# How many loads are issued ahead of the entry barriers in a streaming scale-and-add kernel: three or one

## The chip, the cores and the metric

The kernel runs on one core of one Trainium2 chip. Times are device microseconds of one execution; where a run was timed, the median of its executions is given beside that of the kernel before on the same chip. The profile of an execution counts from the first instruction to the last (the span), and was about 1.3 us shorter than the measured time of the same execution.

## The reference

```python
# x, y: [1024, 16, 512] bf16; gamma: [512] bf16
def reference(x, y, gamma):
    return x + gamma * y
```

Each of x, y and the output is 16.78 MB. Seen as 128 partitions, each partition has 128 rows of 512 elements, 1 KB a row.

## The kernel before

y and x are each loaded in halves of 64 rows per partition. x's buffer in this kernel has 75 rows. Its first half takes 64 of them. The second half comes in two loads: 53 rows overwrite rows of the first half and must wait until VectorE has added these (below, this is "the reload"); the last 11 rows go to a place of their own, but stand behind the reload in the queue. The two queues are written as lists: SP issues loads, ACT issues gamma and the two stores.

```python
PIECES = [53, 11, 53, 11]
SP = [('y', 0, 64), ('x', 0, 64, 0), ('y', 64, 128), ('x', 64, 117, 0), ('x', 117, 128, 64)]
ACT = [('g',), ('s', 0, 64), ('s', 64, 128)]
EARLY = (2, 1)          # how many of SP's and of ACT's issues go ahead of the entry barriers
RELEASE = ('x', 64, 117, 0)
DVE = [('m', 0), ('m', 1), ('a', 0), ('a', 1), ('m', 2), ('m', 3), ('a', 2), ('a', 3)]
```

gamma arrives as one row of 1 KB, is spread to 128 partitions by a matmul with a row of ones, and cast by VectorE:

```python
    nc.vector.memset(ones_row, 1.0).then_inc(s_ones, 1)
    _take(s_ones, 1, nc.tensor)
    _take(s_gamma, 16, nc.tensor)
    nc.tensor.matmul(gamma_ps, ones_row, gamma_row, start=True, stop=True).then_inc(s_ps, 1)
    _take(s_ps, 1, nc.vector)
    nc.vector.tensor_copy(out=gamma_sb, in_=gamma_ps).then_inc(s_dve, 1)
    # ... then VectorE multiplies ('m') and adds ('a') piece by piece
```

At the end of the build, the first issues of each queue are moved to the front of the program, ahead of the barriers that the framework puts at its entry:

```python
            if k < n_early:
                early.append(i.ins)
    # ...
    for k, i in enumerate(early):
        main.insert(1 + k, i)
```

## Time and profile before

| | |
|---|---|
| time, three runs | 119.91 us (119.9 to 120.03) |
| span of the profiled run | 118.6 us |
| both DMA queues, share of 16 engines | 66.0% + 32.6% |
| VectorE busy | 70.0 us, 59% |
| 64 KB packets | 2.418 us each, 48 packets' worth on each DMA engine |

The packets of the two queues fill 98.6% of the 16 engines' span, and VectorE, the busiest of the others, works 59% of it: DMA is the bound. The prediction below shows the page's head and the timeline of the start. The view of waits of the kernel before says who has time to spare. Its columns are: engine, tile and line; what it waited for; us in total, how many times, the longest.

```profile
DVE y_sb L156 <- DVEq L25: 15.4, 2, 13.4
PE gamma_ps L130 <- PEq L25: 7.1, 1, 7.1
...
DVE y_sb L165 <- DVEq L25: 2.2, 1, 2.2
```

L156 is the multiply, L165 the add, L130 the matmul for gamma; L25 is the helper that waits on a semaphore. The first multiply waited 13.4 us although gamma was there, and the first add 2.2 us for x.

### The profile page before, as it was taken

The page shows a single profiled execution, that of the slowest core. Times are in us where ns is not written, and L with a number is a line of the kernel's source. Part 1 is how long each engine was busy: PE and PEld are TensorE (multiplying, and loading weights), DVE is VectorE, ACT ScalarE, POOL GpSimd, SP SyncE. Part 2 cuts the span into 40 slices and gives each one's busy share as a digit, 9 for nine tenths or more (in the row PEclk, how much of TensorE's full clock was granted, in tenths as well). Part 3 has the DMA queues.
Part 4 walks back from the last instruction along what each step waited for, and adds up shares of the span by engine and source line. Part 5 has one row for each costly group of instructions (what it writes and reads, how often), then busy time and mean ns, then how long its engine had stood idle before and what let it go on. Part 6 is the DMA issues. An engine that isn't in the chain of part 4 may idle for free. (4 is left out here: it accounts for less than half of the span.)

```text
span 118.6 us, 78 instructions
## 1 busy us (share of the span) xinstructions
PE 0.6 (0%) x1; PEld 0.1 (0%) x1; DVE 70.0 (59%) x10; POOL 0.2 (0%) x4
## 2 busy tenths in 40 slices
PE   0010000000000000000000000000000000000000
PEld 0000000000000000000000000000000000000000
DVE  0020000699999299999759999999999910000000
POOL 0000000000000000000000000000000000000000
DMA  9889888998899888988896969498899888988892
GB/s 354 354 376 685 354 354 354 641 420 354 354 420 641 354 354 354 685 376 354 354 586 293 586 293 568 201 658 354 354 420 641 354 354 354 708 354 354 354 597 111
DMA packets 1010, 50.33 MB, mean 425 GB/s; under 512 B 113, under 2 KB 114, under 8 KB 114
## 3 DMA queue, kind: packets, MB, share of 16 engines
q1 hardware_dynamic: 720, 33.55, 66.0%
q10 hardware_dynamic: 290, 16.78, 32.6%
HBM read 33.56 MB, written 16.78 MB: 425 GB/s over the span
## 5 line engine op out<-in xcount | busy, mean ns | idle before, releaser
L156 DVE TENSOR_TENSOR y_sb<-y_sb,gamma_sb 128x27136 bf16<-128x27136 bf16 (+1 forms) x4 | 34.6, 8688 | 15.4 <-DVEq L25 15.4
L165 DVE TENSOR_TENSOR y_sb<-x_sb,y_sb 128x27136 bf16<-128x27136 bf16 (+1 forms) x4 | 34.6, 8689 | 2.3 <-DVEq L25 2.2
L132 DVE CAST gamma_sb<-gamma_ps 128x512 bf16<-128x512 f32 x1 | 0.7, 691 | 5.7 <-DVEq L25 5.7
L127 DVE MEMSET ones_row<- 1x128 bf16 x1 | 0.2, 165 | 2.0 <-PEq L41 2.0
L130 PE MATMUL gamma_ps<-gamma_row,ones_row 1*128 1x512 bf16 x1 | 0.6, 580 | 7.1 <-PEq L25 7.1
L130 PEld LDWEIGHTS gamma_ps<-gamma_row,ones_row 1*128 1x128 bf16 x1 | 0.1, 100 | 7.1 <-issue 7.1
L194 POOL MEMSET const-bfloat16-1.0<- 128x1 bf16 x1 | 0.1, 101 | 0.0
L194 POOL MEMSET const-uint8-127<- 128x1 uint8 x1 | 0.1, 101 | 0.0
L194 POOL MEMSET const-float32-0.0<- 128x1 f32 x1 | 0.1, 98 | 0.2 <-issue 0.2
L194 POOL MEMSET const-float32-1.0<- 128x1 f32 x1 | 0.1, 98 | 0.0
## 6 DMA issues: line engine op xcount, KB each, us to landing
x_sb<-in_x_dram SPq DMA_DIRECT2D x1, 6784.0 KB, 20.8
x_sb<-in_x_dram SPq DMA_DIRECT2D x1, 1408.0 KB, 23.8
y_sb<-in_y_dram SPq DMA_DIRECT2D x2, 40.2
out_dram<-y_sb ACTq DMA_DIRECT2D x2, 22.7
gamma_row<-in_gamma_dram ACTq DMA_DIRECT2D x1, 1.0 KB
x_sb<-in_x_dram SPq DMA_DIRECT2D x1, 40.7
```

Of the source, the lines that this page charges most:

```text
L127: nc.vector.memset(ones_row, 1.0).then_inc(s_ones, 1)
L130: nc.tensor.matmul(gamma_ps, ones_row, gamma_row, start=True, stop=True).then_inc(s_ps, 1)
L132: nc.vector.tensor_copy(out=gamma_sb, in_=gamma_ps).then_inc(s_dve, 1)
L156: nc.vector.tensor_tensor(out=yt, in0=yt, in1=g, op=MULT).then_inc(s_dve, 1)
L165: nc.vector.tensor_tensor(out=yt, in0=xt, in1=yt, op=ADD).then_inc(s_add, 1)
L194: nc = _bacc.Bacc("TRN2", target_bir_lowering=False, num_devices=1)
```

## The change

The intent is to keep only what the start needs ahead of the barriers: the first load of y. x's first load and gamma are issued behind them.

```diff
-EARLY = (2, 1)
+EARLY = (1, 0)
```

y's first load is 64 rows of 1 KB on each of 128 partitions, 8.39 MB. By the code of the build, the programs differ only in the place of two DMA instructions (both profiles count 78 instructions): x's load on SP and gamma's on ACT now stand behind the barriers.

## The prediction

> **What bounds the kernel now.** I read the page's head first, then its busy rows, its DMA queues, and the timeline.
>
> ```profile
> span 118.6 us, 78 instructions
> ...
> PE 0.6 (0%) x1; PEld 0.1 (0%) x1; DVE 70.0 (59%) x10; POOL 0.2 (0%) x4
> ...
> DMA  9889888998899888988896969498899888988892
> ...
> q1 hardware_dynamic: 720, 33.55, 66.0%
> q10 hardware_dynamic: 290, 16.78, 32.6%
> HBM read 33.56 MB, written 16.78 MB: 425 GB/s over the span
> ```
>
> The two DMA queues together keep the 16 DMA engines busy for 66.0 + 32.6 = 98.6% of the span; only 1.4% of 118.6 us, about 1.7 us, is free. VectorE, the busiest compute engine, works 59%. So DMA is the bound, and a change of order can save no more than that 1.7 us unless it changes the traffic, which it doesn't. What it can do is open a gap in the traffic. The timeline of the first 10 us shows the part that is edited:
>
> ```profile
> 0.00 0.37 SPq L116 DMA_DIRECT2D y_sb<-in_y_dram  x1
> 0.12 0.52 ACTq L110 DMA_DIRECT2D gamma_row<-in_gamma_dram  x1
> ...
> 0.42 0.42 SPq L113 DMA_DIRECT2D x_sb<-in_x_dram  x1
> 1.90 0.33 SPq L116 DMA_DIRECT2D y_sb<-in_y_dram  x1
> 1.99 0.17 DVE L127 MEMSET ones_row<- 1x128 bf16 x1 [1.99 <-PEq L41]
> 7.07 0.10 PEld L130 LDWEIGHTS gamma_ps<-gamma_row,ones_row 1*128 1x128 bf16 x1 [7.07 <-issue]
> ...
> 7.83 0.69 DVE L132 CAST gamma_sb<-gamma_ps 128x512 bf16<-128x512 f32 x1 [5.67 <-DVEq L25]
> ```
>
> The reader is to see three issues at 0.00, 0.12 and 0.42 us, before the barriers, and the first issue behind them (second half of y) at 1.90. The later timeline shows how late everything else waits:
>
> ```profile
> 21.93 17.29 DVE L156 TENSOR_TENSOR y_sb<-y_sb,gamma_sb 128x27136 bf16<-128x27136 bf16 x2 [13.41 <-DVEq L25]
> 41.38 17.29 DVE L165 TENSOR_TENSOR y_sb<-x_sb,y_sb 128x27136 bf16<-128x27136 bf16 x2 [2.16 <-DVEq L25]
> 55.70 0.81 SPq L113 DMA_DIRECT2D x_sb<-in_x_dram  x2
> ```
>
> VectorE has gamma ready at about 8.5 us (7.83 + 0.69) and then waits 13.41 us more for y; it waits another 2.16 us for x. Neither the second load nor gamma is urgent.
>
> [...] the DMA packet records show SP's packets of y, x, y in strict order, and gamma's one 1 KB packet at 4.17 us, just behind an engine's first y packet, with its semaphore packet one y packet later at 6.63. [...] Here the first y packet starts 1.01 us after its issue[...]. [...] gamma's issue, in the middle of y's, took 0.52 us, and x's 0.42, where issues that stand alone took 0.33 (the second y).
>
> **The ledger of the end.** From the packet records, times from the first issue: the first packets of the 16 engines start at 1.01 to 1.92 us (mean 1.24) and end at 4.00 to 4.55 (mean 4.26). Each engine then carries the rest of 48 packets' worth of 64 KB (8 for each 64-row load, 8 for each 64-row store, six of these), each 2.418 us: 47 x 2.418 = 113.65. 4.26 + 113.65 = 117.91; the last semaphore packets start at 117.82 to 118.16, the final wait passes at 118.56. Packets follow one another within some nanoseconds. So the end is set by when y's first packets finish, plus a fixed amount of traffic, as long as no ring runs dry.
>
> **The change part by part.**
>
> *y's first load* stays the first issue at 0.00. Its first packet should start at 1.01 as before: 0.
>
> *The barriers.* Before, SP reaches the first one only after x's issue ends at 0.84 (its drain ends at 1.03) and ACT after gamma's (0.84); GpSimd, which gathers the others, goes on at 1.05. After, SP's issue ends at 0.37, and with the same 0.055 gap and 0.125 drain it is there at 0.55; GpSimd's own four memsets and drain end at 0.48. So the barriers should open about 0.45 us sooner, at 1.45 in place of 1.90. Nothing that sets the end waits for that: 0.
>
> *x's first load* moves from 0.42 to about 1.45. Its packets stand behind eight y packets per engine; the first x packet started at 20.93. With about 1.0 us from issue to readiness it is ready at 2.5, some 18 us early: 0. y's second load follows 0.4 us behind it, at about 1.85 to 1.9, as before: 0.
>
> *gamma* moves from 0.12 to about 1.5. Ready at about 2.5, it is still ahead of the end of the first y packets (4.00), so its packet may well take the same turn and the matmul stay at 7.1; if it misses one turn, 2.42 us, 9.5. From the end of TensorE's wait for gamma (6.99) to VectorE being free to multiply (8.56) are 1.6 us. y lands at 21.82. So gamma may land as late as 20.2 and cost nothing: 0.
>
> Sum: 0 on the path; 119.9 us as before (the profiled 118.6 plus the 1.3 us by which the measured time exceeds the span).
>
> **The rivals.**
>
> *A: [...]* The first packets take 4.26 - 1.24 = 3.02 us in the mean where later ones take 2.42, so 0.6 us is lost in them, and their starts are staggered by another 0.2. [...] the end moves up by as much as 0.8 us: 119.1. For: x's and gamma's issues lie at 0.12 to 0.84 and 1.01 follows directly. Against: y has the head of the queue[...]. I give it one in five, and a part of the 0.8.
>
> *B: gamma, issued late, is stuck behind packets[...].* At the stores the records show something like it: the first store, issued at 76.89, moved nothing until 79.18, when the small x load before it was through. If gamma waits for all eight y packets, it lands near 21, the multiply starts near 23, and the 2.16 us wait for x absorbs the delay: still 119.9. It costs only when gamma lands after 20.2 + 2.16 = 22.4, and then only once the reload of x, issued at 55.70 and needed at 59.62 when y's last packets run out (slack 59.62 - 55.70 - 1.01 = 2.9 us), is late as well: gamma after 25.3. Stuck behind x too (40.3), it would make 119.9 + 15 = 135. Against: gamma's two packets each waited for one y packet only, with the rings of y and x filled. One in a hundred.
>
> *C: x is issued too late and the engines run dry between y and x.* It would need a delay of 18 us in a barrier that takes 0.9. Nothing speaks for it.
>
> **Range and chances.** The three timed runs of before spread by 0.13 us, and a comparison may drift by twice that. Rival A pulls the low end to 119.4, an unlucky first turn or spread of starts the high end to 120.3. 2% is 2.4 us, more than the whole idle DMA time, so faster by that is next to impossible; slower needs the extreme form of B. Faster 0.005, within 2% 0.98, slower 0.015.
>
> **What would show it.** Right: x's issue at 1.4 to 1.5 and y's second at 1.8 to 1.9; the matmul at 7.1 or one or a few steps of 2.42 later; VectorE's multiply still at 21.9 and its add at 41.4; the reload issue at 55.7; the queues' shares summing to 98 to 99%. Rival A: the first multiply up to 0.8 us earlier, everything behind it shifted by the same, and y's first packets near 2.4 us each. Rival B: the multiply later than 22 and a wait for PE's matmul before it. The prediction is wrong if the DMA row shows a gap near 21 us or 60 us, or if the start of y's first packet moves from 1.01.

Rival A reads: if x's and gamma's issues beside y are what lengthens y's first packets, the end moves up by as much as 0.8 us. "Ring" stands for the waiting packets of one queue. That packets follow one another within some nanoseconds was seen in the trace of the kernel before: in order of time, the 17th start among the packets of y, x and y lies beside the first end, the 18th beside the second and so on, each start from 4 ns before its end to 15 ns after it.

## The result

The changed kernel took 119.98 us (119.9 to 120.09, six runs), the kernel before 120.08 us (119.9 to 120.2, six runs). The ratio is 0.9994, 95% interval 0.9982 to 1.0007: the same. A ratio here and below is the mean time of one kernel's runs over that of the other's of the same rounds, so it is not quite the ratio of the quoted medians.

The head of the changed kernel's page, its DMA row and its queues:

```profile
span 118.6 us, 78 instructions
...
DMA  9889888998899888998896969598899888988892
...
q1 hardware_dynamic: 720, 33.55, 66.0%
q10 hardware_dynamic: 290, 16.78, 32.6%
```

The same span, the same packets and the same shares, and no hole in the DMA row. Its timeline (start, length, engine and line, operation, in brackets the idle time before it; x2 joins two instructions, here one of 53 and one of 11 rows):

```profile
0.00 0.37 SPq L116 DMA_DIRECT2D y_sb<-in_y_dram  x1
...
1.43 0.33 SPq L113 DMA_DIRECT2D x_sb<-in_x_dram  x1
1.43 0.52 ACTq L110 DMA_DIRECT2D gamma_row<-in_gamma_dram  x1
...
1.81 0.45 SPq L116 DMA_DIRECT2D y_sb<-in_y_dram  x1
9.70 0.10 PEld L130 LDWEIGHTS gamma_ps<-gamma_row,ones_row 1*128 1x128 bf16 x1 [9.70 <-issue]
...
21.94 17.29 DVE L156 TENSOR_TENSOR y_sb<-y_sb,gamma_sb 128x27136 bf16<-128x27136 bf16 x2 [10.79 <-DVEq L25]
41.39 17.29 DVE L165 TENSOR_TENSOR y_sb<-x_sb,y_sb 128x27136 bf16<-128x27136 bf16 x2 [2.16 <-DVEq L25]
55.71 0.81 SPq L113 DMA_DIRECT2D x_sb<-in_x_dram  x2
```

x and gamma are issued 1.0 and 1.3 us later than before. The barriers open 0.47 us sooner (1.43 in place of 1.90), because SP no longer reaches them late (its drain ends at 0.55 us in place of 1.03, and GpSimd goes on at 0.58 in place of 1.05). The matmul for gamma comes 2.63 us later, at 9.70. From 21.9 us on, every line stands within 0.02 us of where it stood. The view of waits shows where gamma's delay went:

```profile
DVE y_sb L156 <- DVEq L25: 12.7, 2, 10.8
PE gamma_ps L130 <- PEq L25: 9.7, 1, 9.7
...
DVE y_sb L165 <- DVEq L25: 2.2, 1, 2.2
```

TensorE waits 2.6 us longer for gamma and VectorE 2.6 us shorter for y (13.4 to 10.8). The wait of the add for x is untouched.

### The profile page after: what moved, and what is told of

It reads as the page before. It is cut to its first block, busy times and chain, and to the rows that moved or that the text cites. A ratio compares the mean times of both kernels' runs of the same rounds, so it can differ in the third digit from the quotient of the medians.

```text
span 118.6 us, 78 instructions
## 1 busy us (share of the span) xinstructions
PE 0.6 (0%) x1; PEld 0.1 (0%) x1; DVE 70.0 (59%) x10; POOL 0.2 (0%) x4
## 3 DMA queue, kind: packets, MB, share of 16 engines
q10 hardware_dynamic: 290, 16.78, 32.6%
```

## The experiments

**Theory.** The end is set by the moment at which y's first packets get going plus a fixed amount of DMA traffic. Any other issue is free as long as its packets are ready before the queue's packets ahead of them run out; gamma is free as long as VectorE frees x's buffer in time for the reload. (A queue that has run out is called dry below.) **Rivals.** (A) Other issues beside y's slow y's first packets. (B) gamma's delay is paid for. (C) the second load's issue time is paid for. Line numbers in the experiments' profiles are shifted by the added lines. Diffs are against the changed kernel; in the gated runs `s_gate` is an added semaphore. Lines of a diff that are left out are marked with "...". All runs gave the reference's output.

### None early, and each of the two alone

`e1_none_early`, everything behind the barriers:

```diff
-EARLY = (1, 0)
+EARLY = (0, 0)
```

> No load is ahead of the barriers. Theory (the end is y's first packets plus a fixed amount of traffic): y's first issue moves behind the barriers, which open at about 1.35 us after the place where it stood (1.43 in the changed kernel, less some 0.08 because SP no longer arrives last), so the end moves by the same: 121.3 us, 1.0 to 1.5 us over the kernel before. Gamma and x are then issued right beside y, as in the kernel before. If the idea that they slow y's first packets (rival A) held, those packets would be longer here than in the changed kernel (mean end minus mean start 3.1 us there). If no early issue mattered at all, 119.9 to 120.1.

`e2_gamma_early` has `EARLY = (1, 1)`:

> y and gamma ahead of the barriers, x behind them. Theory: the time of the kernel before within 0.2 us. The barriers open at about 1.7 us (ACT arrives at 0.84), and if the time of its issue decides gamma's turn, the matmul is back at 7.1 us; if it stays at 9.7, the turn is decided by something else. Rival A: gamma's early issue slows y's first packets (mean length over 3.1 us) and the time rises by some tenths over the changed kernel.

`e3_x_early` has `EARLY = (2, 0)`:

> y and x ahead of the barriers, gamma behind them. Theory: the time of the kernel before within 0.2 us; barriers open at 1.9 us as in the kernel before (SP arrives last), gamma is issued at 1.9 and the matmul comes at 9.7 or one turn (2.42 us) later. Rival A: x's early issue slows y's first packets and the time rises by some tenths over the changed kernel.

| run | time, us | ratio to before (95%) | barriers open, us | wait for gamma ends, us | y's first packets, mean length, us |
|---|---|---|---|---|---|
| before | 120.04 | | 1.90 | 6.99 | 3.02 |
| changed (earlier rounds) | 119.98 | 0.9994 (0.9982 to 1.0007) | 1.43 | 9.63 | 3.11 |
| e1_none_early | 121.36 | 1.0111 (1.0098 to 1.0124) | 1.38 | 2.68 | 3.21 |
| e2_gamma_early | 120.10 | 1.0005 (0.9993 to 1.0017) | 1.73 | 7.13 | 3.14 |
| e3_x_early | 119.96 | 1.0001 (0.9988 to 1.0014) | 1.90 | 9.56 | 3.07 |

"Barriers open" is the first issue behind them; the last two columns are from the semaphore and packet records of the trace, the last one over the first packet of each of the 16 DMA engines. The timeline of `e1_none_early`:

```profile
1.38 0.36 SPq L116 DMA_DIRECT2D y_sb<-in_y_dram  x1
1.39 0.53 ACTq L110 DMA_DIRECT2D gamma_row<-in_gamma_dram  x1
...
2.76 0.10 PEld L130 LDWEIGHTS gamma_ps<-gamma_row,ones_row 1*128 1x128 bf16 x1 [2.76 <-issue]
...
23.36 17.29 DVE L156 TENSOR_TENSOR y_sb<-y_sb,gamma_sb 128x27136 bf16<-128x27136 bf16 x2 [19.15 <-DVEq L25]
```

y is issued 1.38 us later, the multiply starts 1.42 us later than in the changed kernel, and the time is 1.3 us longer. So being early is worth the whole barrier time, but only to the first load. gamma, whose packet here started 0.93 us after the issue, was there by 2.68 us, four to seven us earlier than in the other four kernels of the table, and that bought nothing. Putting either of the two other issues back ahead of the barriers left it within 0.05% of the kernel before. Rival A falls: y's first packets are not shorter where less is issued beside them. They take 3.02 us in the kernel before and 3.11 in the changed kernel, whose other issues at 1.43 to 1.81 still fall within y's first packets; in `e5_x_after_y` below, with nothing but gamma's 1 KB issued beside y in the first 22 us, they take 3.15. They take 3.02 us or more in all five kernels of the table, for another reason, which no run shows.

### How late may x be?

`e4_x_after_cast` holds x's first load until VectorE has cast gamma:

```diff
             elif kind == "x":
+                if w[1] == 0:
+                    _take(s_gate, 1, eng)
     ...
     nc.vector.tensor_copy(out=gamma_sb, in_=gamma_ps).then_inc(s_dve, 1)
     _take(s_dve, 1, nc.vector)
+    nc.vector.sem_inc(s_gate, 1)
```

> As the changed kernel, but SP also waits with x's first load (and y's second behind it) until VectorE has cast gamma, so x is issued near 11.3 us in place of 1.43. Theory: x need only be ready when y's packets run out at 20.9 us, so a delay of ten more us still costs nothing: the time of the kernel before within 0.2 us, x's landing unchanged near 41.3 us. Rival C (the second load's issue time is on the path): some 10 us longer.

`e5_x_after_y` holds it until y's first load has landed (the same wait, and the increment behind VectorE's wait for that load, ahead of the first multiply):

```diff
             need(y_loads, c)
+            if c == 0:
+                nc.vector.sem_inc(s_gate, 1)
```

> As the changed kernel, but SP waits with x's first load until VectorE has seen y's first load land, so x is issued near 22.0 us, after y's packets ran out (20.9 to 21.5). Theory (an issue is free as long as it is ready before the ring runs dry): now there is a gap. If the restart is as slow as the start (first packets end 4.3 us after their issue, as in the changed kernel), x's first packets end at 26.3 in place of 23.6, so the time is 2.7 us longer: 122.6. If the slow first packets are special to the start of the program, they end at 22.0 + 1.2 + 2.4 = 25.6: 2.0 us longer, 121.9. If the second load's place did not matter at all: 120.

`e4_x_after_cast` took 120.03 us beside 120.04 (ratio 1.0004, 0.9992 to 1.0016). `e5_x_after_y` took 122.58 beside 120.00 (1.0217, 1.0201 to 1.0234). The timeline of `e4_x_after_cast`, x's issue and the add that uses it:

```profile
11.31 0.33 SPq L116 DMA_DIRECT2D x_sb<-in_x_dram  x1
...
41.37 17.29 DVE L169 TENSOR_TENSOR y_sb<-x_sb,y_sb 128x27136 bf16<-128x27136 bf16 x2 [2.14 <-DVEq L25]
```

and the same two of `e5_x_after_y`:

```profile
22.09 0.33 SPq L116 DMA_DIRECT2D x_sb<-in_x_dram  x1
...
44.06 17.30 DVE L170 TENSOR_TENSOR y_sb<-x_sb,y_sb 128x27136 bf16<-128x27136 bf16 x2 [4.68 <-DVEq L25]
```

An issue at 11.31 us, ten us later than in the changed kernel, leaves the add at 41.37. An issue at 22.09 moves it by 2.67 us, and the time by 2.58. Rival C falls, and so does the idea that the second load has no deadline: it has one between 11.3 and 22.1 us. Estimated from the packet records it lies near 20 us (y's packets run out from 20.9 us on, and the first packet came 0.95 us after the issue); no run tried that place. The packet records of `e5_x_after_y` also say what the restart cost beside the gap itself. x's first packets took 3.10 us in the mean, where they took 2.42 in the changed kernel, right behind y's. They ended at 26.31 us in the mean (26.3 was expected) against 23.65 in the changed kernel.

### How late may gamma be?

`e6_gamma_after_y` holds gamma until y's first load has landed, so VectorE's wait for y goes ahead of its wait for the matmul:

```diff
             if kind == "g":
+                _take(s_gate, 1, eng)
     ...
+    _take(s_load[('y', 0, 64)], 16, nc.vector)
+    nc.vector.sem_inc(s_gate, 1)
     _take(s_ps, 1, nc.vector)
     ...
```

> As the changed kernel, but ACT waits with gamma until y's first load has landed, so gamma is issued near 22.0 us and has to take its turns among x's packets: landing between 26 and 30 us. The prediction put the free limit at 25.3 us, with the cost after that one for one. Theory: the multiply starts 1.65 us after the landing, at 28 to 32, the reload of x is issued at 60 to 63.5 in place of 55.7, y's packets run out before it at about 60, and the time is 122 to 125.5 us. Rival (gamma is so small that it never matters): 119.9 to 120.1.

`e7_gamma_delay_a` holds gamma until VectorE has done 40 memsets of the gamma buffer; `e8_gamma_delay_18` and `e9_gamma_delay_10` do 18 and 10.

```diff
             if kind == "g":
+                _take(s_gate, 1, eng)
     ...
+    for k in range(40):
+        nc.vector.memset(gamma_sb, float(k)).then_inc(s_dve, 1)
+        _take(s_dve, 1, nc.vector)
+    nc.vector.sem_inc(s_gate, 1)
```

> As the changed kernel, but ACT waits with gamma until VectorE has done 40 small memsets (each waited for), so gamma is issued somewhere between 10 and 19 us and lands between 16 and 25 us. Theory: as long as the landing is before 25.3 us the time is that of the kernel before within 0.2 us, even where the multiply starts later than 21.94. Rival (every delay of the multiply is paid for): longer by the time that the multiply starts after 21.94.

> The same delay with 18 memsets; the run with 40 issued gamma at 32.6 us, so one memset with its wait took 0.77 us and this issue comes near 15.6, the landing (6.6 to 8.3 us after the issue in the runs so far) at 22.2 to 23.9 and the multiply at 23.8 to 25.6, later than the 21.94 of the changed kernel. Theory: still free, because the two late runs (landing 28.7 and 40.9 us, 4.2 and 16.5 us longer) both point to a limit of 24.4 us: 119.9 to 120.2, with the wait of the first add for x shrunk from 2.16 us to nothing. Rival (every delay of the multiply is paid for): 121.9 to 123.7.

> The same delay with 10 memsets: gamma issued near 9.4 us, landing at 16.0 to 17.7, multiply still at 21.94. Theory: 119.9 to 120.2, nothing behind 21.9 us moved. Rival (gamma's place among the packets matters whatever its landing): some other time.

The dose of `e7_gamma_delay_a` was misjudged. One memset with its wait took 0.77 us, not the 0.2 to 0.45 that the expectation implied, so gamma was issued at 32.6 us. The run still gives a point, far out on the paid side. `e8_gamma_delay_18` was 0.37 us longer than before, which neither theory had expected, so two runs made the same delay with fewer, longer instructions. Their diff is that of above with 10 memsets of a scratch buffer of 1200 columns (`e11_gamma_wide_a`) and 11 of 1312 columns (`e12_gamma_wide_b`).

> The run with 18 memsets was 0.37 us longer than the kernel before, although its adds still waited 0.85 us for x; its trace has one 8 KB instruction packet inside the span (at 100.8 us) on one DMA engine, whose next store packet took 2.89 in place of 2.42 us, and the runs without it lost nothing. Here the same delay is made of 10 longer memsets in a scratch buffer, gamma issued near 15 us, the multiply again near 23.4. Theory (the delay is free, the 0.37 us is the longer program's instruction fetch): no instruction packet in the span, 119.9 to 120.2. Rival (a later multiply costs a little): again 120.3 to 120.5.

> The same with 11 memsets of 1312 columns: gamma issued near 17.5 us, landing one turn later near 24.1, the multiply near 25.8, almost at the limit. Theory: the add for x then waits for the multiplies and ends at 57.4 (55.7 in the changed kernel), the reload of x is issued there and its first packet is due at 58.5, still ahead of 59.6 where y's packets run out: 119.9 to 120.2. If the limit is lower than the 25.3 us of the prediction by more than a microsecond: up to 121. Rival (every delay of the multiply is paid for): 123.8.

All in one table. "Landed" is the end of TensorE's wait for gamma; the last two columns are the issue of x's reload, and the mean end of its first packets on the 16 engines.

| run | gamma issued | landed | first multiply | first add | reload issued | reload's first packets end | time (before beside it) | ratio (95%) |
|---|---|---|---|---|---|---|---|---|
| changed | 1.43 | 9.63 | 21.94 | 41.39 | 55.71 | 61.91 | 119.98 (120.08) | 0.9994 (0.9982 to 1.0007) |
| e9_gamma_delay_10 | 9.14 | 16.86 | 22.05 | 41.49 | 55.80 | 61.92 | 119.99 (119.99) | 1.0001 (0.9988 to 1.0013) |
| e8_gamma_delay_18 | 15.28 | 21.66 | 23.45 | 41.59 | 55.91 | 61.90 | 120.36 (119.99) | 1.0033 (1.0021 to 1.0046) |
| e11_gamma_wide_a | 16.58 | 21.84 | 23.62 | 41.40 | 55.72 | 61.93 | 120.07 (120.08) | 1.0006 (0.9992 to 1.0019) |
| e12_gamma_wide_b | 19.33 | 26.54 | 28.33 | 45.77 | 60.09 | 63.95 | 122.04 (120.08) | 1.0165 (1.0151 to 1.0179) |
| e6_gamma_after_y | 22.07 | 28.71 | 30.38 | 47.82 | 62.14 | 65.93 | 124.17 (120.00) | 1.0348 (1.0331 to 1.0366) |
| e7_gamma_delay_a | 32.63 | 40.90 | 42.69 | 60.13 | 74.45 | 78.26 | 136.56 (120.00) | 1.1379 (1.1362 to 1.1396) |

The decisive pair is `e11_gamma_wide_a` and `e12_gamma_wide_b`. The timeline of the first, multiply, add and reload:

```profile
23.62 17.29 DVE L163 TENSOR_TENSOR y_sb<-y_sb,gamma_sb 128x27136 bf16<-128x27136 bf16 x2 [0.26 <-DVEq L25]
41.40 17.29 DVE L172 TENSOR_TENSOR y_sb<-x_sb,y_sb 128x27136 bf16<-128x27136 bf16 x2 [0.48 <-DVEq L25]
55.72 0.81 SPq L116 DMA_DIRECT2D x_sb<-in_x_dram  x2
```

and of the second:

```profile
28.33 17.29 DVE L163 TENSOR_TENSOR y_sb<-y_sb,gamma_sb 128x27136 bf16<-128x27136 bf16 x2 [0.26 <-DVEq L25]
45.77 17.29 DVE L172 TENSOR_TENSOR y_sb<-x_sb,y_sb 128x27136 bf16<-128x27136 bf16 x2
60.09 0.80 SPq L116 DMA_DIRECT2D x_sb<-in_x_dram  x2
```

In the first, the multiply is 1.68 us later than in the changed kernel, the add's wait for x shrinks by the same 1.68 (2.16 to 0.48), and everything behind stands still: no cost. In the second, the wait is used up (no bracket on the add), the reload is issued 4.38 us later, and its first packets end 2.05 us later (63.95 less 61.91). The time grew by 1.96. For the other two late runs the same subtraction gives 4.02 and 16.35 us against 4.17 and 16.56 measured. So what gamma's delay costs is what reaches the reload, to within about 0.2 us.

`e12_gamma_wide_b` landed a turn later than its expectation had it (each memset with its wait took 1.60 us), beyond the limit and not just short of it, so it is one more point on the paid side. The strip between 21.84 and 26.54 us was not tried.

**The 0.37 us of `e8_gamma_delay_18`.** The DMA row of its page and that of `e11_gamma_wide_a` differ in one packet. First the run with 18 memsets:

```profile
DMA packets 1011, 50.34 MB, mean 423 GB/s; under 512 B 113, under 2 KB 114, under 8 KB 114
```

then the run with 10:

```profile
DMA packets 1010, 50.33 MB, mean 424 GB/s; under 512 B 113, under 2 KB 114, under 8 KB 114
```

The packet records name it: an instruction packet of 8 KB at 100.85 us, 0.31 us long, on an engine whose next store packet then took 2.89 us in place of 2.42. (The records do not name a packet's engine; it is inferred from which packet starts where another ends.) That engine lost 0.31 + 0.47 = 0.78 us, and it ended last: the last semaphore packets (of 4 bytes, behind the data; in the kernel before the last 16 start at 117.82 to 118.16 us, and the last 16 counts of the stores' semaphore stand at 118.18 to 118.53) start at 117.70 to 118.52 us, against 117.64 to 118.22 in the changed kernel. With ten memsets the packet is absent and so is the cost. The later multiply is not to blame: the reload's first packets end at 61.90 us, as in the changed kernel (61.91). Some of the loss is not the packet's, though. Less the 0.78 us, that engine would have ended near 117.74, but another one, whose first packet took 3.63 us, ended at 118.31 anyway. So in this one trace the packet accounts for about 0.2 us; that it explains all of the 0.37 us is not shown. The trace of `e7_gamma_delay_a` has such a packet too, at 28.52 us; its engine lost 0.86 us to it, but then stood idle until the late reload and was among the first to end.

### Can the slow start be bought off?

The one loss seen at the start is the slow first packets. `e10_small_first` splits y's first load:

```diff
-SP = [('y', 0, 64), ('x', 0, 64, 0), ...
+SP = [('y', 0, 8), ('y', 8, 64), ('x', 0, 64, 0), ...
-EARLY = (1, 0)
+EARLY = (2, 0)
```

> y's first load in two parts, 8 rows and then 56, both ahead of the barriers; x and gamma behind them. The first packets of every start and restart so far took 3.1 us for 64 KB where later ones take 2.42. Theory (a fixed 0.7 us of latency at a cold start): a first packet of 8 KB takes about 0.3 + 0.7 us and the time stays within 0.2 us of the kernel before. Rival (the slow rate lasts as long as the first packet, in proportion to its size): the loss shrinks to a fraction and the time falls by 0.5 to 0.7 us, below both kernels.

It took 119.85 us beside 119.99, ratio 0.9988 with an interval of 0.9974 to 1.0002: not told apart from the kernel before. The first 8 KB packets took 0.77 us in the mean where the settled ones of that load took 0.31, so some 0.46 us are lost even on a small packet, beside 0.69 on one of 64 KB (3.11 less 2.42, in the changed kernel). y's last packets ran out at 20.85 to 21.47 us, against 20.95 to 21.46. Most of the loss was there at an eighth of the size, and small first packets did not buy it off. No version that beats both kernels was found.

## Why the prediction was right

**The ledger of the end** held: y's first packets ended at 4.32 us in the mean (4.26 before), and the last semaphore packets started at 117.64 to 118.22 us. `e1_none_early` is its direct test: with the first term moved by 1.38 us, the time moved by 1.3.

**The barriers**: predicted to open at 1.45 us, x and gamma to be issued at about 1.45 and 1.5, y's second load at 1.85 to 1.9. Measured 1.43, 1.43, 1.43 and 1.81. That nothing waits for them is shown by `e2_gamma_early` and `e3_x_early`, which open them at 1.73 and 1.90 in the same time.

**x's margin of 18 us**: ten of them were used up free of charge by `e4_x_after_cast`, and that there is a deadline was shown by `e5_x_after_y`.

**gamma's turn**: here a step was off. The prediction thought that the matmul might well stay at 7.1 us, because gamma would be ready at 2.5, ahead of the end of the first y packets; it came at 9.70, its second choice. gamma was probably ready on time (in `e1_none_early` its packet started 0.93 us after the issue), but in the eleven runs that issued it at 1.4 us or later with y's first issue at 0.00 (all but the kernel before, e1 and e2) its packet started 3.5 to 5.4 us after the issue. Less the 0.93, that is 2.6 to 4.5 us, always more than one large packet (2.42 us; 2.12 in e10, where they were of 56 KB) and less than two. So gamma let a whole further packet go first in these runs. That reading of the numbers is an inference, and why it is so was not shown. The slip cost nothing, because the first multiply still had 10.8 us to wait for y.

**The length of an issue.** The prediction set gamma's issue of 0.52 us, in the middle of y's, against the 0.33 of an issue that stands alone. Its place is not the reason: gamma's issue took 0.52 to 0.53 us in every run, also with no other issue near it (at 16.58 us in `e11_gamma_wide_a`). Nothing in the sum rested on it.

**gamma's limit of 25.3 us** was right to within about 0.1 us, worked back from the three runs past it (no run landed near it). The reload's first packets started, in the mean, 1.33, 3.39 and 15.69 us later than in the changed kernel in the three late runs; the landings lie 1.24, 3.41 and 15.60 past 25.3. The term that was missing is the restart. "One for one past the limit" leaves out that a queue which ran dry restarts slowly: in the three late runs the reload's first packets took 2.64 to 2.73 us in place of 2.00, another 0.6 to 0.7 us each time. The 24.4 us in the expectation of `e8_gamma_delay_18`, worked back from the times without this term, was too low for that reason.

**Rival A** was given one chance in five; it fell. **Rival B** was rightly called cheap in its mild form, and `e12_gamma_wide_b`, `e6_gamma_after_y` and `e7_gamma_delay_a` show that its costly form is real but needs gamma some 17 us later than here. The 135 us worked out for a landing at 40.3 has its counterpart in `e7_gamma_delay_a`: 136.56 for a landing at 40.90, the restart included. **Rival C** fell.

What stays open is why first packets are slow. It isn't special to the program's start, since x's load in `e5_x_after_y` (3.10 us in place of 2.42) and the late reloads (2.64 to 2.73 in place of 2.00) show much the same loss; the runs don't say what it consists of.

## What to carry to other kernels

In this kernel the two queues' packets fill 98.6% of the 16 engines' span, and only the very first issue had to be early: 1.38 us later cost 1.3 us. A later load on the same queue had a deadline, estimated as the time at which the packets ahead of it run out, less the 1 us or so from its issue to its first packet (0.95 in `e5_x_after_y`): x's issue at 11.31 us was free, at 22.09 it cost 2.58. gamma's deadline came from the engine that uses it: a landing at 21.84 us was free, at 26.54 it cost 1.96. Work the deadlines out from the trace before moving anything: here a load of 1 KB among 64 KB packets of 2.42 us started 3.5 to 5.4 us after its issue, against 0.93 in `e1_none_early`, and the wait for it ended 5.3 to 8.3 us after the issue. A queue that had run dry cost the gap and, in these runs, another 0.6 to 0.7 us in its first packets.
